# A four-slot PSUM ring, decoding in the units with values, two buffers for R, and the first x in parts: one change to an attention and feed-forward kernel

## The chip, the cores and the metric

The kernel runs on one core of one Trainium2 chip. A core has a matrix engine (TensorE, PE in the profile; PEld is its weight load), VectorE (DVE), ScalarE (ACT), GpSimd (POOL) and SyncE (SP), which here issues DMAs. They run side by side and wait for each other through semaphores. SBUF is the working memory; PSUM takes what PE computes, in 8 banks of 512 float32 a partition, and is read by DVE and ACT.

The metric is the device time of one execution in microseconds. Before the change it is 735.52 us, the median of 3 runs (735.19 to 736.1).

## The reference

Four batches of eight heads of attention, in which a query sees only the keys that fall into the same bucket of a six-bit hash; then a feed-forward block with a convolution along the sequence and a gate:

```python
# q, k, v: (4, 8, 768, 64), proj: (64, 6), w_in: (512, 1024), conv_w: (3, 1024), w_out: (1024, 512)
q_bits = (np.einsum('bhsd,dk->bhsk', q, proj) > 0)      # the same for k; six bits make a bucket
mask = q_bucket[:, :, :, None] == k_bucket[:, :, None, :]
scores = np.where(mask, q @ k.T / 8, -1000000000.0)
attn = np.exp(scores - scores.max(-1))
attn = attn / (attn.sum(-1) + 1e-09)
x = (attn @ v).transpose(0, 2, 1, 3).reshape(B, S, 512)
h = np.maximum(x @ w_in, 0.0)
conv_out = sum(conv_w[k] * hp[:, k:k + S] for k in range(3))   # hp: h with a zero row at each end
return (h * sigmoid(conv_out)) @ w_out
```

[...]

## The kernel before, in words

**Attention.** The 32 heads are taken in 16 pairs (`Pair`). A pair has 12 units (`Unit`): two heads times six tiles of 128 queries. One loop (L460) runs over all 192 units, and four iterations more; with i its index, `pi` is the pair and `k` = 0 to 11 the unit in it. An iteration writes down, in the order in which every engine then executes it:

- PE: the scores s of unit i (`products`, L274; four matmuls, 128 x 768 in two banks), and the transposes t of unit i-4 (`transposes`, L309; six, in two banks).
- DVE: the maximum of unit i (`maximum`, L292), which reads s from PSUM and leaves e in SBUF, and small operations on sums (L303, L296, L306).
- ACT: the copy of t of unit i-4 to SBUF (`to_sbuf`, L319), then the exponential of unit i (L299).
- POOL: the normalisation of unit i-1 (L307). The last matmul of s of unit i waits for the normalisation of unit i-4, so that the transposes behind it find it done.

Every fourth iteration (k = 0, 4, 8) PE also multiplies four units' weights with v (`values`, L322: 24 matmuls into one bank). Its result is copied to SBUF by DVE and stored to a scratch tensor xd in DRAM by the function `out`, which the loop calls in the next iteration, behind that iteration's maximum. This stretch of four units and one v is called a group below.

**The next pair** is prepared in the units k = 1 to 7 of the pair before (`prepare`, L225): POOL splits its R (768 columns of q and k, two heads) into a high and a low part (L198, L203), SP moves the parts to their places, PE computes the hash bits from R (L213, k = 3), DVE and POOL turn them into rows of ones and zeros (L216, L218). R has one buffer: the load of the pair after next, at k = 7, waits until nothing reads the old R.

**PSUM.** s, t and hash take turns in a ring of three slots of two banks (tag S); v, and later h, in a ring of two single banks (tag M). A tile is written only when all that read the slot's previous tile are done.

**Decoding the weights** (`split_weights`, L103) goes on beside attention: 16 blocks of 128 x 512, four DVE steps each (two `upper`, two `lower`), two ACT operations (L86, L132) and three of POOL (L89, L117, L119). From unit 10 on, three of four iterations take one step of it; a block lasts some 11 units. ACT fetches one raw block every six units (L168).

**The feed-forward part** (`feed_forward`, L415) begins in the loop's last iterations. For each of 4 batches, 2 halves of the sequence and 8 chunks f of the inner dimension PE computes h (L350, 12 matmuls), ACT and DVE the Relu, the convolution, the sigmoid and the product (L355 to L363), ACT and POOL split the result in two (L368, L369), and PE, three chunks later, multiplies it with w_out (o, L399, nine matmuls) into three slots of the S ring. Its input x comes back from xd; the four parts of the first batch are loaded at pair 6 and split by POOL (L387, L389) in pairs 9 and 10.

The constants that set this order:

```python
DECODE, RATE = 10, 0.75
FETCH = 6
X0, X0_SPLIT = 6, 9
```

Of the kernel before, what the change touches and what calls it, by code (L numbers as in the profile page):

```python
# [34 lines left out]
PREP_N = 6  # L35
DECODE, RATE = 10, 0.75
FETCH = 6
X0, X0_SPLIT = 6, 9
WC = 512
# [3 lines left out]
def lsh_attention_conv_ffn(ctx, tc, qk, v, hw, w_in, conv_w, w_out, consts, ident_in, out):  # L43
# [5 lines left out]

    turns = {}  # L50

    def ring(pool, bufs, shape, dtype, tag, name):

        k = turns[tag] = (turns.get(tag, -1) + 1) % bufs
        return pool.tile(shape, dtype, tag=f"{tag}{k}", name=name, bufs=1)


# [45 lines left out]
    def split_weights():  # L103

        todo, ends = [], iter(())

        def ahead():  # L110
            if fetched:
                raw, name = fetched.pop(0)
                todo.append(Decode(raw, WC, name))
                todo[-1].size()

        def finish(d, blk):
            nc.gpsimd.tensor_tensor(d.upf, d.upf, blk[:, 0, :].bitcast(F32), ALU.subtract)  # L117
            yield
            nc.gpsimd.tensor_tensor(blk[:, 1, :], d.upf, d.lowf, ALU.add)  # L119

        ahead()
        yield
        todo[-1].clamp()
        yield
        while todo:
            d = todo.pop(0)
            steps = [*d.upper(), *d.lower()]
            for k, step in enumerate(steps):
                step()
                if k == 3:  # L130
                    blk = weights[d.name] = cp.tile([P, 2, WC], F32R, tag=f"w{d.name}", name=f"w{d.name}")
                    nc.scalar.copy(blk[:, 0, :], d.upf)  # L132
                yield
                if k < 2:
                    next(ends, None)
                elif k == 2:
                    ahead()
                elif todo:
                    todo[-1].clamp()
                yield  # L140
            ends = finish(d, blk)

        for _ in ends:
            yield

    def decode_taps(raw):
# [26 lines left out]
    class Pair:  # L173
# [3 lines left out]
        def load(self):  # L177
            nm = self.nm
            self.R = ring(wp, 1, [P, 2, S], F32R, "R", f"R{nm}")
            src = qk[self.b, 2 * self.p:2 * self.p + 2].rearrange("h p s -> p h s")  # L180
            if self.b == self.p == 0:
                for h in range(2):
                    nc.sync.dma_start(self.R[:, h].bitcast(F32), src[:, h])
            else:
                nc.sync.dma_start(self.R.bitcast(F32), src)
            self.Q1 = ring(wp, 2, [P, 2, S], F32R, "Q1", f"Q1{nm}")
            self.K1 = ring(wp, 2, [P, 2, S], F32R, "K1", f"K1{nm}")
            self.Q2, self.K2 = Q2s[self.p % 2], K2s[self.p % 2]
# [18 lines left out]
        def hash(self):  # L207
            hp = ring(ps, 3, [P, 2, 512], F32, "S", f"hash{self.nm}")
            R = self.R.bitcast(F32)
# [23 lines left out]
        def prepare_now(self):  # L233
# [3 lines left out]
            for h in range(2):  # L237
                hps.append(ring(ps, 2, [P, 512], F32, "M", f"hash{nm}_{h}")[:, :HS])
# [29 lines left out]
    class Unit:  # L268
# [5 lines left out]
        def products(self, w):  # L274

            pr, h = self.pair, self.h
            qs = slice(self.t * P, (self.t + 1) * P)
            self.sp = ring(ps, 3, [P, 2, 512], F32, "S", f"s{self.nm}")
            for kk, (A, C) in enumerate(((pr.Q1, pr.K1), (pr.Q2, pr.K2))):
# [29 lines left out]
        def transposes(self):  # L309
            self.tp = ring(ps, 3, [P, 2, 512], F32, "S", f"t{self.nm}")  # L310
            for c in range(NCK):
# [10 lines left out]
    def values(pr, qb, ats):  # L322

        av = ring(ps, 2, [P, 512], F32, "M", f"v{pr.nm}_{qb}")
        for c in range(NCK):
# [11 lines left out]

    g2, prep, acc = [None], [iter(())], []
    xd = [[tc.dram_tile([P, S], F32, name=f"xd{b}_{c}") for c in range(NCC)] for b in range(B)]

    def hidden(b, half, f, xs):
        c0 = 0 if half == 0 else S - HW
        hp = ring(ps, 2, [P, 512], F32, "M", f"h{b}_{half}_{f}")
        n = 0
# [25 lines left out]

    def load_x(b):

        xs = []
        for c in range(NCC):
            if b % 2 == 0:
                x = ring(wp, NCC, [P, 2, S], F32R, "x", f"x{b}_{c}")
            else:
                x = ring(wp, 2, [P, 2, S], F32R, ("Q1", "K1")[c % 2], f"x{b}_{c}")
            nc.sync.dma_start(x[:, 1].bitcast(F32), xd[b][c])
            xs.append(x)  # L380
        return xs

    def split_x(xs):

# [30 lines left out]
    def feed_forward(x0):  # L415

        gs, run, xs, splits = [], [], x0, iter(())
        load_table(AF.Sigmoid)
        todo = [(b, half, f) for b in range(B) for half in range(2) for f in range(NFC)]
        per = 2 * NFC  # L420
        for i in range(len(todo) + FLAG):
            if i % per == 0 and i < len(todo):
                if i:
                    xs = nxt
                if i // per + 1 < B:
                    nxt = load_x(i // per + 1)
                    splits = split_x(nxt)
            if i < len(todo):
                run.append(hidden(*todo[i], xs))
                next(run[i])  # L430
            if 1 <= i <= len(todo):
                next(run[i - 1], None)
            if i == 0:
                acc.extend(ring(ps, 3, [P, 2, 512], F32, "S", f"o{k}") for k in range(3))
            if i >= FLAG:
# [21 lines left out]
    pairs[1].load()  # L457
    n, tail, x0 = len(units), None, None
    outs, av, splits, due = [], None, iter(()), 0
    for i in range(n + LAG + 1):  # L460
# [8 lines left out]
        elif prev:  # L469
            prev.total()  # L470
        for o in outs:
            o()
        outs = []
        if w:
# [11 lines left out]
        if av:  # L486
            outs.append(values(*av))
            av = None
            if i >= n:
                outs.pop()()  # L490
        if burst:
            av = w.pair, w.qb, w.pair.at
        if u and k == PREP + PREP_N and pi + 1 < len(pairs):
            pairs[pi + 1].load_v()
            if pi + 2 < len(pairs):
                pairs[pi + 2].load()
        if i == 3:
            taps.append(decode_taps(cwr))
        for g in taps:
            next(g, None)  # L500
        if i % FETCH == FETCH - 1:
            fetch(1)
        if i >= DECODE:
            due += RATE
            if due >= 1:
                due -= 1
                next(weights_todo, None)
        if pi == X0 and k == 0:
            x0 = load_x(0)
            splits = split_x(x0)  # L510
        if pi >= X0_SPLIT and k % 3 == 2:
            next(splits, None)
        if i == n:
            tail = feed_forward(x0)
        if tail:
            next(tail)
    for o in outs:
        o()
    for _ in tail:
# [44 lines left out]
```

## Time and profile before

| What | Value |
|---|---|
| median of 3 runs | 735.52 us |
| the profiled execution | 732.21 us |
| its span (first to last instruction) | 730.4 us |
| mean granted TensorE clock | 0.993 |
| PE busy | 703.3 us, 96% |
| DVE busy | 497.3 us, 68% |
| ACT busy | 485.6 us, 66% |
| POOL busy | 451.0 us, 62% |
| HBM read and written | 63 GB/s over the span |

The summary of the profile lists the busy time of each engine in 40 equal slices, in tenths:

```profile
PE   5999999999999999999999999999999999999997
DVE  7776767777767777767677764567567666756563
ACT  5778778777778777768777776555455454545553
POOL 4765876876967979996877853365246325622221
```

The first 25 slices are attention, the rest the feed-forward part. All four engines are well loaded in attention.

How to read the rows: a row of a timeline has the start in us from the span's start, the duration in us, the engine, the line, the operation, the tiles (written <- read), their shapes and a count; in square brackets stands how long the engine was idle before and what ended that. A row of a group has the count, the total in us and the mean in ns, then the idle time before such instructions in us. A row of the table of waits has total, times and longest, in us.

### The profile page before, as it was taken

The numbers are of one execution on the slowest core, as the hardware profiler recorded it, in microseconds if no ns is written. First come the engines' busy times: TensorE is split into PE (matmuls) and PEld (weight loads), VectorE is DVE, ScalarE is ACT, GpSimd is POOL, SyncE is SP. The second block draws the span as 40 slices with busy tenths as digits, with TensorE's granted clock in tenths as the row PEclk, the third lists the DMA queues.
The fourth block names the chain that finished last, engine by engine and source line by source line (L and its number), as shares of the span: only waits on it lengthen the run. The fifth ranks groups of instructions, "written<-read, shape, count | busy, mean of one in ns | idle before, by whom it ended". The sixth has DMA issues, their size and how long they took to land.

```text
span 730.4 us, 13371 instructions
## 1 busy us (share of the span) xinstructions
PE 703.3 (96%) x4552; PEld 589.4 (81%) x4552; DVE 497.3 (68%) x1303; ACT 485.6 (66%) x892; POOL 451.0 (62%) x422
## 2 busy tenths in 40 slices
PE   5999999999999999999999999999999999999997
PEld 2877778877877787778777788799989899899896
DVE  7776767777767777767677764567567666756563
ACT  5778778777778777768777776555455454545553
POOL 4765876876967979996877853365246325622221
PEclk7999999999999999999999999999999999999999
DMA  3666676677876555465565512001210120101011
GB/s 115 170 205 184 168 207 190 165 213 215 225 212 190 141 151 159 112 179 159 120 173 158 138 52 99 11 1 44 87 44 15 51 108 1 44 0 44 1 44 43
DMA packets 39572, 84.76 MB, mean 116 GB/s; under 512 B 6960, under 2 KB 14672, under 8 KB 39504
## 3 DMA queue, kind: packets, MB, share of 16 engines
q1 hardware_dynamic: 36912, 75.47, 37.1%
q10 hardware_dynamic: 2592, 8.44, 3.5%
q8 instruction: 36, 0.59, 0.3%
q14 instruction: 32, 0.26, 0.1%
HBM read 33.70 MB, written 12.58 MB: 63 GB/s over the span
## 4 chain that ended last, share of the span: by engine, by line
PE 76%; DVE 10%; DMA 4%; ACT 4%; POOL 3%; issue 2%; SPq 1%; ACTq 0%; POOLq 0%; DVEq 0%
PE o L399 18%; PE h L350 18%; PE v L327 16%; PE s L281 12%; PE t L312 10%; DVE e L292 5%; DMA R<-in_qk 3%; PE hash L213 2%; POOL e L307 2%; ACT at L319 1%; ACT e L299 1%; DMA k<-R 1%; DVE x L332 1%; POOL R L203 1%; DVE ht L359 1%
## 5 line engine op out<-in xcount | busy, mean ns | idle before, releaser
L292 DVE TENSOR_SCALAR_CACHE_REDUCE e<-s 128x768 f32<-128x768 f32 x192 | 182.5, 950 | 84.9 <-PE s L281 84.5
L307 POOL TENSOR_SCALAR e<-e,st 128x768 f32<-128x768 f32 x192 | 186.4, 974 | 86.8 <-DVE st L306 77.5
L319 ACT COPY at<-t 128x768 f32<-128x768 f32 x192 | 152.3, 793 | 87.1 <-PE t L312 87.1
L299 ACT ACTIVATE e<-e,st 128x768 f32<-128x768 f32 x192 | 180.6, 941 | 12.7 <-DVE st L306 7.7
L369 POOL TENSOR_TENSOR g<-ht,g 128x384 fp32r<-128x384 f32 x64 | 69.7, 1089 | 165.8 <-ACT g L368 133.5
L312 PE MATMUL t<-ident,e 128*128 128x128 f32 x1152 | 159.5, 275 | 7.8 <-DVE e L292 4.9
L359 DVE SCALAR_TENSOR_TENSOR ht<-ht,cw 128x384 f32<-128x384 f32 (+1 forms) x128 | 119.3, 932 | 66.9 <-ACT ht L357 64.5
L312 PEld LDWEIGHTS t<-ident,e 128*128 128x128 f32 x1152 | 134.5, 141 | 22.2 <-DVE e L292 15.1
L350 PE MATMUL h<-x,wi 128*128 128x386 f32 x768 | 146.0, 339 | 0.0
L399 PE MATMUL o<-wo,g 128*128 128x512 f32 x576 | 143.6, 394 | 0.0
L350 PEld LDWEIGHTS h<-x,wi 128*128 128x128 f32 x768 | 136.4, 188 | 5.8 <-issue 0.8
L327 PE MATMUL v<-at,v 128*64 128x256 f32 x1152 | 137.0, 383 | 1.6 <-ACT at L319 1.5
L399 PEld LDWEIGHTS o<-wo,g 128*128 128x128 f32 x576 | 107.3, 188 | 20.5
L281 PE MATMUL s<-K,Q 128*128 128x384 f32 x384 | 116.9, 386 | 2.2 <-POOL K L247 1.2
L327 PEld LDWEIGHTS v<-at,v 128*64 128x64 f32 x1152 | 87.4, 137 | 37.7 <-issue 7.9
L281 PE MATMUL s<-k,q 96*128 96x384 f32 x384 | 100.7, 342 | 3.2 <-DVE e L292 2.1
L362 ACT ACTIVATE ht<-ht 128x384 f32<-128x384 f32 x64 | 33.7, 526 | 97.0 <-DVE ht L359 97.0
L281 PEld LDWEIGHTS s<-K,Q 128*128 128x128 f32 x384 | 58.6, 192 | 32.6 <-issue 18.0
L281 PEld LDWEIGHTS s<-k,q 96*128 96x128 f32 x384 | 70.8, 191 | 5.4 <-ACT q L260 3.1
L363 DVE TENSOR_TENSOR ht<-ht 128x384 f32<-128x384 f32 x64 | 47.4, 741 | 33.7 <-ACT ht L362 33.7
L203 POOL TENSOR_TENSOR R<-R,hi 128x768 fp32r<-128x768 f32 x30 | 55.1, 1836 | 0.0
L355 ACT ACTIVATE ht<-h 128x386 f32<-128x386 f32 x64 | 31.6, 495 | 32.6 <-PE h L350 32.6
(65 smaller groups left out, 523.1 us busy)
## 6 DMA issues: line engine op xcount, KB each, us to landing
R<-in_qk SPq DMA_DIRECT2D x15, 768.0 KB
K<-hi SPq DMA_DIRECT2D x60, 192.0 KB
v<-in_v SPq DMA_DIRECT2D x16, 384.0 KB
xd<-x SPq DMA_DIRECT2D x48, 128.0 KB
x<-xd SPq DMA_DIRECT2D x16, 384.0 KB
out<-osb SPq DMA_DIRECT2D x24, 256.0 KB
Q<-hi SPq DMA_DIRECT2D x30, 192.0 KB
q<-hi SPq DMA_DIRECT2D x30, 192.0 KB
```

The source lines that it names most:

```text
L203: nc.gpsimd.tensor_tensor(lo, R, hi.bitcast(F32), ALU.subtract)
L281: mm = nc.tensor.matmul(self.sp[:, half, :HS], A[:, h, qs], C[:, h, half * HS:(half + 1) * HS], start=(kk == 0), stop=(kk == 1))
L292: nc.vector.tensor_scalar(self.e.rearrange("p (a b) -> p a b", a=2), self.sp[:, :, :HS], MASKED, None, ALU.max, ALU.max, accum_out=self.st ...
L299: nc.scalar.activation(self.e, self.e, AF.Exp, bias=self.st[:, 1:2], scale=SCALE, accum_out=self.st[:, 2:3])
L307: self.norm = nc.gpsimd.tensor_scalar(self.e, self.e, self.st[:, 3:4], 0.0, ALU.mult, ALU.add)
L312: nc.tensor.transpose(self.tp[:, c // 3, c % 3 * P:(c % 3 + 1) * P], self.e[:, c * P:(c + 1) * P], ident)
L319: nc.scalar.copy(pr.at[self.h][:, :, :, self.tq * P:(self.tq + 1) * P], self.tp[:, :, :3 * P].rearrange("p j (c q) -> p j c q", c=3))
L327: nc.tensor.matmul(av[h * D:(h + 1) * D, :QB], pr.v[:, c, h, :], ats[h][:, c // 3, c % 3, :], start=(c == 0), stop=(c == NCK - 1), tile_po ...
L350: nc.tensor.matmul(hp[:, :HW], w, x[:, c0:c0 + HW], start=(n == 0), stop=(n == 3 * NCC - 1))
L359: nc.vector.scalar_tensor_tensor(t[:, a:z], ht[:, o + k - 1 + a:o + k - 1 + z], cw[:, f, k:k + 1], t[:, a:z], ALU.mult, ALU.add)
L369: nc.gpsimd.tensor_tensor(g[:, 1, :], t, g[:, 0, :].bitcast(F32), ALU.subtract)
L399: nc.tensor.matmul(op, l, r, start=(f == 0 and i == 0), stop=(f == NFC - 1 and i == 2))
```

## The change

1. The S ring of three and the M ring of two become one ring of four slots of two banks (`slot`). s, t, hash and now v take the slots in turn. The feed-forward part keeps one slot for h (`keep=True`; chunk f uses bank f % 2 of it, so h is one tile from then on), and takes two for o when the first o is due and the third eight chunks later.
2. A block of weights is decoded in 8 units. Both `upper` steps stand in one iteration and both `lower` steps in another four units on, and these are iterations with a v (i a multiple of 4). One raw block is fetched every eight units, three units before it is first used.
3. The copy of v and its store are written down in v's own iteration, behind the decode steps, and not in the next.
4. R has two buffers. The load of the pair after next stands at k = 8, and the load of v at k = 10.
5. The four parts of the first x are loaded one a pair in pairs 10 to 13 (k = 9), and split one a pair in pairs 11 to 14, half at k = 8 and half at k = 10.

The diff, cut to its core:

```diff
-DECODE, RATE = 10, 0.75
-FETCH = 6
-X0, X0_SPLIT = 6, 9
+DECODE = FETCH = 8
+X0 = 10
...
+    slots = list(range(4))
...
+    def slot(name, keep=False):
+
+        k = slots.pop(0)
+        if not keep:
+            slots.append(k)
+        return ps.tile([P, 2, 512], F32, tag=f"S{k}", name=name, bufs=1)
...
         while todo:
             d = todo.pop(0)
-            steps = [*d.upper(), *d.lower()]
-            for k, step in enumerate(steps):
+            for step in d.upper():
                 step()
...
+            ahead()
+            yield
+            if todo:
+                todo[-1].clamp()
+            yield from rest(DECODE // 2 - 1)
+            for step in d.lower():
+                step()
+            blk = weights[d.name] = cp.tile([P, 2, WC], F32R, tag=f"w{d.name}", name=f"w{d.name}")
+            nc.scalar.copy(blk[:, 0, :], d.upf)
+            yield
+            nc.gpsimd.tensor_tensor(d.upf, d.upf, blk[:, 0, :].bitcast(F32), ALU.subtract)
+            yield
+            nc.gpsimd.tensor_tensor(blk[:, 1, :], d.upf, d.lowf, ALU.add)
+            yield from rest(DECODE // 2 - 2)
...
-            self.R = ring(wp, 1, [P, 2, S], F32R, "R", f"R{nm}")
+            self.R = ring(wp, 2, [P, 2, S], F32R, "R", f"R{nm}")
...
-            hp = ring(ps, 3, [P, 2, 512], F32, "S", f"hash{self.nm}")
+            hp = slot(f"hash{self.nm}")
...
-            self.sp = ring(ps, 3, [P, 2, 512], F32, "S", f"s{self.nm}")
+            self.sp = slot(f"s{self.nm}")
...
-            self.tp = ring(ps, 3, [P, 2, 512], F32, "S", f"t{self.nm}")
+            self.tp = slot(f"t{self.nm}")
...
-        av = ring(ps, 2, [P, 512], F32, "M", f"v{pr.nm}_{qb}")
+        av = slot(f"v{pr.nm}_{qb}")[:, 0]
...
-        hp = ring(ps, 2, [P, 512], F32, "M", f"h{b}_{half}_{f}")
+        hp = hps[0][:, f % 2]
...
+        hps.append(slot("h", keep=True))
...
-            if i == 0:
-                acc.extend(ring(ps, 3, [P, 2, 512], F32, "S", f"o{k}") for k in range(3))
+            if i == FLAG:
+                acc.extend(slot(f"o{k}", keep=True) for k in range(2))
+            if i == FLAG + NFC:
+                acc.append(slot("o2", keep=True))
...
-        for o in outs:
-            o()
-        outs = []
...
-        if u and k == PREP + PREP_N and pi + 1 < len(pairs):
+        if u and k == PREP + PREP_N + 1 and pi + 2 < len(pairs):
+            pairs[pi + 2].load()
+        if u and k == PREP + PREP_N + 3 and pi + 1 < len(pairs):
             pairs[pi + 1].load_v()
-            if pi + 2 < len(pairs):
-                pairs[pi + 2].load()
...
-        if i % FETCH == FETCH - 1:
+        if i % FETCH == FETCH - 3:
             fetch(1)
         if i >= DECODE:
-            due += RATE
-            if due >= 1:
-                due -= 1
-                next(weights_todo, None)
-        if pi == X0 and k == 0:
-            x0 = load_x(0)
-            splits = split_x(x0)
-        if pi >= X0_SPLIT and k % 3 == 2:
-            next(splits, None)
+            next(weights_todo, None)
+        if X0 <= pi < X0 + NCC and k == 9:
+            x0.append(load_x(0, pi - X0))
+        if X0 < pi <= X0 + NCC and k in (8, 10):
+            if k == 8:
+                splits = split_x(x0[pi - X0 - 1])
+            next(splits)
+        if out_x:
+            out_x()
+            out_x = None
```

Three places in the built order. The first is DVE around a v of pair 3 of the first batch (iteration i = 40, k = 4), before; e is written by the maximum, wl and wu belong to a decoded block, x is the copy of v:

```order
L292 TENSOR_SCALAR e_3_2_0_1291,st_3_2_0_1290<-s_3_2_0_1285 128x768
L303 TENSOR_SCALAR st_3_1_1_1258<-st_3_1_1_1258 128x1
L296 TENSOR_SCALAR st_3_2_0_1290<-st_3_2_0_1290 128x1
L306 RECIPROCAL st_3_1_1_1258<-st_3_1_1_1258 128x1
L100 TENSOR_SCALAR wli_0_1053<-wui_0_1052 128x512
L292 TENSOR_SCALAR e_3_3_0_1337,st_3_3_0_1336<-s_3_3_0_1331 128x768
L303 TENSOR_SCALAR st_3_2_0_1290<-st_3_2_0_1290 128x1
L296 TENSOR_SCALAR st_3_3_0_1336<-st_3_3_0_1336 128x1
L332 COPY x_2_2_1341<-v_2_2_1317 128x256
L306 RECIPROCAL st_3_2_0_1290<-st_3_2_0_1290 128x1
```

The same place now:

```order
L295 TENSOR_SCALAR e_3_2_0_1299,st_3_2_0_1298<-s_3_2_0_1293 128x768
L306 TENSOR_SCALAR st_3_1_1_1267<-st_3_1_1_1267 128x1
L299 TENSOR_SCALAR st_3_2_0_1298<-st_3_2_0_1298 128x1
L309 RECIPROCAL st_3_1_1_1267<-st_3_1_1_1267 128x1
L101 TENSOR_SCALAR wli_0_1096<-wli_0_1096 128x512
L102 SCALAR_TENSOR_TENSOR wui_0_1095<-rawi_0_1004,wli_0_1096 128x512
L335 COPY x_2_2_1343<-v_2_2_1325 128x256
L295 TENSOR_SCALAR e_3_3_0_1352,st_3_3_0_1351<-s_3_3_0_1346 128x768
```

Two decode steps stand together ahead of the copy of v, and the copy ahead of the next maximum. Before, the next decode step (L101) stood three units on, among the units without a v.

The second place is PE in the third unit after that v, with the semaphores that each row waits for, before:

```order
L281 MATMUL s_3_3_1_1387<-K_3_688,Q_3_687 128x384 [waits Activation_49]
L281 MATMUL s_3_3_1_1387<-K_3_688,Q_3_687 128x384
L281 MATMUL s_3_3_1_1387<-k_1_76,q_1_74 128x384 [waits DMAHW3_49]
L281 MATMUL s_3_3_1_1387<-k_1_76,q_1_74 128x384 [waits Pool_49]
L312 MATMUL t_3_1_1_1397<-ident,e_3_1_1_1259 128x128 [waits DVE_49]
L312 MATMUL t_3_1_1_1397<-ident,e_3_1_1_1259 128x128 x5
L281 MATMUL s_3_4_0_1420<-K_3_688,Q_3_687 128x384 [waits Activation_49]
```

And now:

```order
L284 MATMUL s_3_3_1_1395<-K_3_724,Q_3_723 128x384 [waits DVE_49]
L284 MATMUL s_3_3_1_1395<-K_3_724,Q_3_723 128x384
L284 MATMUL s_3_3_1_1395<-k_1_76,q_1_74 128x384
L284 MATMUL s_3_3_1_1395<-k_1_76,q_1_74 128x384 [waits Pool_49]
L315 MATMUL t_3_1_1_1405<-ident,e_3_1_1_1268 128x128 [waits Activation_49]
L315 MATMUL t_3_1_1_1405<-ident,e_3_1_1_1268 128x128 x5
L284 MATMUL s_3_4_0_1419<-K_3_724,Q_3_723 128x384 [waits DVE_49]
```

Before, s waited for ACT's copy of an earlier t, and t for DVE's maximum of the unit just before. Now s waits for the maximum of the unit two before, and t for ACT's copy of the t two before it.

The third place is SP's queue at the start, before:

```order
L183 DMA R_0_97<-in_qk 128x768 x2
L451 DMA ident<-in_ident 128x128
L192 DMA v_0_103<-in_v 128x768
L454 DMA cwr<-in_conv_w 128x48
L185 DMA R_1_134<-in_qk 128x2x768 [waits DMAHW1_49,DVE_49,DMAHW3_49,PE_49,Activation_49]
```

And now:

```order
L186 DMA R_0_97<-in_qk 128x768 x2
L454 DMA ident<-in_ident 128x128
L195 DMA v_0_103<-in_v 128x768
L457 DMA cwr<-in_conv_w 128x48
L188 DMA R_1_134<-in_qk 128x2x768
```

The load for the second pair waited for three engines and two earlier transfers, and now for nothing.

More of the change, by code (lines that the diff above doesn't have):

```diff
@@ L103, in split_weights @@
     def split_weights():
-        todo, ends = [], iter(())
+        todo = []
         def ahead():
@@ L114, in ahead, with rest @@
                 todo[-1].size()
-        def finish(d, blk):
+        def rest(n):
+            return (None for _ in range(n))
+        ahead()
+        yield
+        todo[-1].clamp()
+        yield from rest(DECODE - 1)
+        while todo:
+            d = todo.pop(0)
+            for step in d.upper():
+                step()
+            ahead()
+            yield
+            if todo:
+                todo[-1].clamp()
+            yield from rest(DECODE // 2 - 1)
+            for step in d.lower():
+                step()
+            blk = weights[d.name] = cp.tile([P, 2, WC], F32R, tag=f"w{d.name}", name=f"w{d.name}")
+            nc.scalar.copy(blk[:, 0, :], d.upf)
+            yield
             nc.gpsimd.tensor_tensor(d.upf, d.upf, blk[:, 0, :].bitcast(F32), ALU.subtract)
@@ L119, in finish @@
             nc.gpsimd.tensor_tensor(blk[:, 1, :], d.upf, d.lowf, ALU.add)
[L121 to L126, printed above, removed]
-            steps = [*d.upper(), *d.lower()]
-            for k, step in enumerate(steps):
[L129 to L144, printed above, removed]
+            yield from rest(DECODE // 2 - 2)
     def decode_taps(raw):
@@ L237, in prepare_now @@
             for h in range(2):
-                hps.append(ring(ps, 2, [P, 512], F32, "M", f"hash{nm}_{h}")[:, :HS])
+                hps.append(slot(f"hash{nm}_{h}")[:, 0, :HS])
                 for g in range(4):
@@ L335, in values @@
         return out
-    g2, prep, acc = [None], [iter(())], []
+    g2, prep, acc, hps = [None], [iter(())], [], []
     xd = [[tc.dram_tile([P, S], F32, name=f"xd{b}_{c}") for c in range(NCC)] for b in range(B)]
@@ L369, in hidden, with load_x, split_x @@
         nc.gpsimd.tensor_tensor(g[:, 1, :], t, g[:, 0, :].bitcast(F32), ALU.subtract)
[L371 to L383, printed above, removed]
+    def load_x(b, c):
+        if b % 2 == 0:
+            x = ring(wp, NCC, [P, 2, S], F32R, "x", f"x{b}_{c}")
+        else:
+            x = ring(wp, 2, [P, 2, S], F32R, ("Q1", "K1")[c % 2], f"x{b}_{c}")
+        nc.sync.dma_start(x[:, 1].bitcast(F32), xd[b][c])
+        return x
+    def split_x(*xs):
         for x in xs:
@@ L425, in feed_forward @@
                 if i // per + 1 < B:
-                    nxt = load_x(i // per + 1)
-                    splits = split_x(nxt)
+                    nxt = [load_x(i // per + 1, c) for c in range(NCC)]
+                    splits = split_x(*nxt)
             if i < len(todo):
@@ L457, in lsh_attention_conv_ffn @@
     pairs[1].load()
-    n, tail, x0 = len(units), None, None
-    outs, av, splits, due = [], None, iter(()), 0
+    n, tail, x0 = len(units), None, []
+    out_x, av, splits = None, None, iter(())
     for i in range(n + LAG + 1):
@@ L486, in lsh_attention_conv_ffn @@
         if av:
-            outs.append(values(*av))
+            out_x = values(*av)
             av = None
-            if i >= n:
-                outs.pop()()
         if burst:
             av = w.pair, w.qb, w.pair.at
-        if u and k == PREP + PREP_N and pi + 1 < len(pairs):
+        if u and k == PREP + PREP_N + 1 and pi + 2 < len(pairs):
+            pairs[pi + 2].load()
+        if u and k == PREP + PREP_N + 3 and pi + 1 < len(pairs):
             pairs[pi + 1].load_v()
-            if pi + 2 < len(pairs):
-                pairs[pi + 2].load()
         if i == 3:
@@ L516, in lsh_attention_conv_ffn @@
             next(tail)
-    for o in outs:
-        o()
     for _ in tail:
```

## The prediction

> **What bounds the kernel now.** I read the summary first (the table above), then the timeline of single engines in the attention stage, then the chain of waits, then the table of waits. PE looks full in the summary, but the ends of its rows are modelled, so its share hides gaps. The question is how far its pace lies from the densest pace that it shows. One group of four units (scores s and transposes t each, then one product with the values, v) runs like this where nothing holds it up, PE alone:
>
> ```profile
> 192.91 2.81 PE L327 MATMUL v<-at,v 128*64 128x256 f32 x24
> 195.65 0.61 PE L281 MATMUL s<-K,Q 128*128 128x384 f32 x2
> 196.10 0.51 PE L281 MATMUL s<-k,q 96*128 96x384 f32 x2
> 196.45 0.82 PE L312 MATMUL t<-ident,e 128*128 128x128 f32 x6
> 197.03 0.60 PE L281 MATMUL s<-K,Q 128*128 128x384 f32 x2
> ...
> 201.34 2.00 PE L327 MATMUL v<-at,v 128*64 128x256 f32 x16
> ```
>
> Start to start, v takes 2.74 us, s 0.80, t 0.58, and v returns after 201.34 - 192.91 = **8.43 us**. The v rows of the chain of waits give the real pace:
>
> ```profile
> 27.30 2.74 PE v L327 x24
> ...
> 119.54 2.74 PE v L327 x24
> 128.91 2.74 PE v L327 x24
> ...
> 438.63 2.80 PE v L327 x24
> ```
>
> There are 48 v (16 pairs, three each). From the first to the 46th are 45 intervals in 411.33 us, 9.14 each. Fourteen of them hold the hash of the next pair; one of those, among the shortest, is 128.91 - 119.54 = 9.37. At the dense pace the 45 would take 31 x 8.43 + 14 x 9.37 = 392.5. So **18.8 us** is all that better overlap can win here. Who holds PE up:
>
> ```profile
> PEld t L312 <- DVE e L292: 15.1, 24, 1.6
> ...
> PE hash L213 <- DMA R<-in_qk: 2.4, 3, 1.3
> ```
>
> The columns are total, times and longest, in us; PEld is the weight load, which meets a stall first. Transposes that wait for the maximum of the unit before are by far the greatest of these waits. One such place, all engines:
>
> ```profile
> 78.19 0.41 DVE L332 COPY x<-v 128x256 f32<-128x256 f32 x1
> ...
> 78.56 1.28 POOL L119 TENSOR_TENSOR wi<-wui,wli 128x512 fp32r<-128x512 f32 x1
> 78.59 1.54 DVE L100 TENSOR_SCALAR wli<-wui 128x512 int32<-128x512 int32 x1
> ...
> 81.06 0.33 PE L312 MATMUL t<-ident,e 128*128 128x128 f32 x1 [1.26 <-DVE e L292]
> ```
>
> A decode step, itself held beside a POOL operation that began just before it, sits on DVE ahead of a maximum. The maximum is late, and the transposes that take over its slot in the ring of three stand for 1.26 us.
>
> The feed-forward stage, from some 465 us, is another matter:
>
> ```profile
> 469.86 2.10 PE o L399 x9
> 471.96 2.12 PE h L350 x12
> ```
>
> ```profile
> ACT ht L355 <- PE h L350: 32.6, 61, 2.1
> ```
>
> PE alternates h and o without a gap, and ACT waits for PE 61 times. Nothing can be won there.
>
> **The change part by part.** No instruction goes or comes: each engine has as many rows in the order as before. Only places and waits differ.
>
> *Ring of four.* Before, transposes waited for the maximum one unit back: 0.58 + 0.80 = 1.38 us of PE work lie between, and DVE needs 0.94 plus what is queued ahead of it. Now scores wait for the maximum two units back, with 0.58 + 0.80 + 0.58 = 1.96 between, and every second pair of transposes for a copy of ACT, with 2.18 between. The v shares the ring, and waits for DVE or ACT work at least as old.
>
> *Decoding beside v.* DVE's free time around a v, where no decode lies:
>
> ```profile
> 439.72 0.17 DVE L306 RECIPROCAL st<-st 128x1 f32<-128x1 f32 x1
> 442.38 0.96 DVE L292 TENSOR_SCALAR_CACHE_REDUCE e<-s 128x768 f32<-128x768 f32 x1 [2.50 <-PE s L281]
> ```
>
> It is free for 2.49 us. The copy of v (0.41 at 78.19) now stands ahead of the next maximum and can begin when v is done; so two decode steps have 2.49 - 0.41, about 2.1 us. Their price, by the dearer group of each line of a block's first half:
>
> ```profile
> L95 DVE SCALAR_TENSOR_TENSOR wui<-rawi,wli 128x512 int32<-128x512 int32 x8 | 10.2, 1279 | 0.0
> ...
> L94 DVE TENSOR_SCALAR wlo<-wlo 128x512 int32<-128x512 int32 x8 | 5.8, 721 | 3.4 <-POOL wlo L89 3.4
> ```
>
> That half costs 1.28 + 0.72 = 2.00; the other half, two operations of the same kinds and shape, I take at the same. It fits, barely, and these means hide a spread:
>
> ```profile
> 193.90 2.18 DVE L95 SCALAR_TENSOR_TENSOR wui<-rawi,wli 128x512 int32<-128x512 int32 x1
> ```
>
> This one took 0.9 more than its line's mean. Such a step late in v's shadow delays the next maximum, exponential and copy, and v itself. The Trainium skill, "SBUF — State Buffer", section "Who interferes with whom", has a rule for it: DVE and GpSimd share one pair of ports, and whichever starts second is blocked until the other's instruction ends. The rows at 78.56 and 78.59 agree with it. By that rule both steps of a unit could be held in turn; if that happened in every unit as at 78.59, the sum below would be +12 instead of -16.5, which is the slower rival.
>
> I take 0.1 us lost in each of the 32 units with decoding (16 blocks, two halves): **3.2 us** given back. The low bound is nothing, since the means fit; the high one is the slower rival's 32.
>
> ACT's part of decoding (one operation of a block's two in such a unit) falls into ACT's idle time at v:
>
> ```profile
> 197.31 0.80 ACT L319 COPY at<-t 128x768 f32<-128x768 f32 x1 [2.09 <-PE t L312]
> ...
> 200.55 0.79 ACT L319 COPY at<-t 128x768 f32<-128x768 f32 x1
> ```
>
> 2.09 us hide an operation on 512 columns, where the copy of 768 takes 0.80: nothing. The raw block is now fetched three units ahead of its first use, some 5 us at the 3.24 us that ACT takes from its copy at 197.31 to the second next at 200.55. If it came later, the remaining 1.3 us of idle time would still cover it; beyond that each us costs 16, once a block.
>
> *Two buffers for R.* The load for pair 1 no longer waits for the first pair's reads:
>
> ```profile
> 12.69 0.39 SPq L185 DMA_DIRECT2D R<-in_qk  x1
> ...
> 16.97 1.51 PE L213 MATMUL hash<-R,hw_sb 128*32 128x384 f32 x8 [1.27 <-DMA R<-in_qk]
> ```
>
> It is now free to be issued right behind the first loads, some 9 us earlier, and lands, by the same 4.28 us, long before the hash: **-1.3 us**, between 0 (another wait behind it) and 2. Later loads lose the wait for their predecessor's DMAs; what that wins (the 2.4 us of the DMA row above) lies within the 18.8.
>
> *x a part a pair.* Splits move from pairs 9 and 10, where they met decoding, to pairs 11 to 14, two POOL operations a pair. What this wins is in the 18.8 too. What hides the splits is the distance of four units between a unit's scores and its transposes; where POOL ran so late that this was used up, the split of a part would cost some 2 us by the POOL operation on two inputs of the same size (1.28 for 512 columns, so 1.9 for 768), 8 for the four.
>
> *One tile for both halves of h.* In the built order h now waits for the Relu of the chunk just before, not of the one before that. The transition, where no o stands between them yet:
>
> ```profile
> 460.31 0.49 ACT L355 ACTIVATE ht<-h 128x386 f32<-128x386 f32 x1
> ...
> 464.74 2.81 PE L327 MATMUL v<-at,v 128*64 128x256 f32 x22 [1.54 <-ACT at L319]
> ```
>
> In the steady stage the o between two h (2.10) covers a Relu of 0.49, which starts as h ends: nothing. Here the fourth h would start after 460.31 + 0.49 = 460.8 instead of earlier; with h 2.12 and o 2.10 behind it the last v starts near 465.1 instead of 464.74: **+0.4 us**, because v waited there anyway.
>
> Sum: -18.8 + 3.2 - 1.3 + 0.4 = **-16.5 us**. The profiled execution took 732.21 us, of which the span is 730.4; it would become 715.7. The median of the timed runs, 735.52, lies 3.3 above it, so the forecast in their terms is 735.52 - 16.5 = **719.0 us**.
>
> **The rivals.** *ACT takes DVE's place.* In the dense group above, the third copy ends at 200.55 + 0.79 = 201.34, just as v starts, and v needs it. PE cannot outrun ACT there, and whatever delays the first exponential of a group delays v as much. For it: no slack at all. Against it: 8.43 was reached while decoding was in progress. At 0.25 us a group it takes back 45 x 0.25 = 11.3: 730.3 us.
>
> *The decoding jams v.* Both steps of every unit with decoding start just behind a POOL operation and take 1.54 us, as at 78.59. Together 3.1 us, they overrun the 2.1 by 1.0, 32 times: 32 us against a gain of 19.7 without the 3.2, so 735.5 + 12.3 = 748 us. The kernel gets slower from a mean of 2.1 + 19.7 / 32 = 2.7 us a unit. For it: in the built order POOL has its split of R, its longest operation in a pair, in the unit ahead of two of a pair's three v. Against it: the same steps beside the same POOL work average 2.0 now. The rule of "SBUF — State Buffer" in the Trainium skill that is weighed above speaks for this rival; the row at 78.59 bears it out for a single step only.
>
> *The stalls only move.* If PE waits for POOL's normalisation or for SP's transfers instead, the time stays at 735.5. Against it: the table of waits names few of either.
>
> **How the numbers follow.** Forecast, 712 to 724: 0.64. ACT takes over, 724 to 734: 0.20. Stalls move, within 734 to 737: 0.06. Jam, over 737: 0.10. The low end of the range is the full 18.8 + 1.3 and 2 us more from shorter hash intervals, 713; the high end takes in the rival of ACT with 2 us to spare, 732. Outside are the jam, the unmoved time and thin edges, 0.2 in all. A measurement of this kernel can tell about 0.2%, 1.5 us, from no change; by that, faster 0.84, same 0.06, slower 0.10.
>
> **What would show it.** Right: the waits of t for DVE e fall from 15.1 us to under 4; v returns every 8.4 to 8.6 us, and 9.4 with a hash; the two decode steps stand between the reciprocal and the copy of v and together take about 2 us; the second load of R is issued near 3 us and no hash waits for it; h and o keep 2.12 and 2.10. Wrong: waits of v for ACT's copy in tenths of a us per group (first rival); decode rows near 2 us each with v late behind them (jam); waits of s for POOL e grow (third). If the feed-forward stage stretched, the reading of the shared h tile would be wrong.

## The result, and the profile after

| | before | after |
|---|---|---|
| median | 735.81 us (735.19 to 736.13, 4 runs) | 723.37 us (722.6 to 724.71, 4 runs) |
| ratio, 95% interval | | 0.9843 (0.9821 to 0.9866) |
| the profiled execution | 732.21 us | 723.74 us |
| its span | 730.4 us | 722.0 us |
| first v starts | 27.23 us | 26.36 us |
| 31 intervals from v to v without a hash | 273.6 us, 8.83 each | 262.8 us, 8.48 each |
| 14 intervals with a hash | 137.7 us, 9.84 each | 140.6 us, 10.04 each |
| from the 47th v to the end of the span | 284.0 us | 284.4 us |

The last four rows are taken from the starts of v on PE's timeline and make up the span, but for the one interval from the 46th v to the 47th, 7.8 us in both. They are used for every kernel below: *dense* are the intervals without a hash, *hash groups* those with one.

Now line 284 is the scores, 295 the maximum, 315 the transposes, 322 ACT's copy of them, 330 v, 335 the copy of v, and 101 to 108 are the decode steps on DVE, which turn the two 32-bit words of each float64 weight into float32 parts. The timeline of PE after the change, v alone:

```profile
26.36 3.15 PE L330 MATMUL v<-at,v 128*64 128x256 f32 x24
...
44.55 2.81 PE L330 MATMUL v<-at,v 128*64 128x256 f32 x24
52.90 2.37 PE L330 MATMUL v<-at,v 128*64 128x256 f32 x19
...
114.72 3.29 PE L330 MATMUL v<-at,v 128*64 128x256 f32 x24
124.99 2.81 PE L330 MATMUL v<-at,v 128*64 128x256 f32 x24
...
429.79 2.94 PE L330 MATMUL v<-at,v 128*64 128x256 f32 x24
```

A dense group is now as short as 52.90 - 44.55 = 8.35. But a hash group stands at 124.99 - 114.72 = 10.27, where the shortest of its kind take 9.35. The 45 intervals sum to 403.4 us, against 411.3. The table of waits, weight loads and matmuls:

```profile
PEld v L330 <- ACT at L322: 2.9, 8, 0.6
...
PEld t L315 <- DVE bits L219: 0.2, 1, 0.2
```

```profile
PE s L284 <- DMA Q<-R: 1.9, 2, 1.6
...
PE s L284 <- DMA k<-R: 1.0, 2, 0.6
```

The 15.1 us of transposes that waited for a maximum are gone; the only wait of t for DVE left is 0.2 us. Grown are the waits of v for ACT's copy: from their start to the next scores the first 46 v take 132.3 us, and before the change 126.9. Where nothing holds a v it takes 2.74. New are waits of scores for the low parts of R. The second kind, PE and then SP's queue in one place:

```profile
172.45 0.82 PE L315 MATMUL t<-ident,e 128*128 128x128 f32 x6
174.88 0.59 PE L284 MATMUL s<-K,Q 128*128 128x384 f32 x2 [1.61 <-DMA Q<-R]
176.10 0.62 PE L284 MATMUL s<-k,q 96*128 96x384 f32 x2 [0.63 <-DMA k<-R]
```

```profile
163.77 0.71 SPq L225 DMA_DIRECT2D q<-bits  x1
164.59 0.45 SPq L336 DMA_DIRECT2D xd<-x  x1
165.49 0.53 SPq L204 DMA_DIRECT2D Q<-hi  x1
166.07 0.58 SPq L204 DMA_DIRECT2D q<-hi  x1
166.70 1.52 SPq L204 DMA_DIRECT2D K<-hi  x2
168.33 0.88 SPq L208 DMA_DIRECT2D Q<-R  x1
169.25 0.86 SPq L208 DMA_DIRECT2D k<-R  x1
170.16 0.59 SPq L188 DMA_DIRECT2D R<-in_qk  x1
```

POOL has had this low part since 163.48 (the row of L206 further down). SP issues it only at 168.33, behind eight DMAs of bits (the last is shown), a store and four DMAs of the high part; the scores wait for it until 174.88. Low parts that SP issues 2.2 to 5.8 us after POOL had them lie behind every second pair (the odd ones, from pair 1 to pair 11). Against 9.35, these six hash groups are 9.3 us too long in sum. Of that, 3.2 us are v's wait for ACT's copy, 0.4 to 0.7 in each. Behind pairs 1 and 11 it is nearly all of the excess, and no score waits for a low part there; the other 6.1 us lie behind pairs 3, 5, 7 and 9.

### The profile page after: what moved, and what is told of

Its sections match the earlier page's. It is cut to its first block, busy times and chain, and to the rows that moved or that the text cites. A ratio compares the mean times of both kernels' runs of the same rounds, so it can differ in the third digit from the quotient of the medians.

```text
span 722.0 us, 13429 instructions
## 1 busy us (share of the span) xinstructions
PE 702.4 (97%) x4552; PEld 598.8 (83%) x4552; DVE 523.1 (72%) x1303; ACT 485.5 (67%) x892; POOL 449.6 (62%) x422
## 4 chain that ended last, share of the span: by engine, by line
PE 86%; DVE 3%; DMA 3%; ACT 3%; POOL 2%; issue 2%; SPq 0%; POOLq 0%; ACTq 0%; DVEq 0%
PE h L353 19%; PE o L399 19%; PE s L284 17%; PE v L330 16%; PE t L315 14%; DMA k<-R 3%; PE hash L216 2%; ACT e L302 1%; POOL e L310 1%; DVE e L295 1%; ACT at L322 1%; POOL R L206 1%; DMA R<-in_qk 0%; DVE Q L254 0%; DVE k L259 0%
## 5 line engine op out<-in xcount | busy, mean ns | idle before, releaser
L310 POOL TENSOR_SCALAR e<-e,st 128x768 f32<-128x768 f32 x192 | 181.5, 949 | 82.8 <-PE s L284 31.9
L372 POOL TENSOR_TENSOR g<-ht,g 128x384 fp32r<-128x384 f32 x64 | 69.4, 1084 | 166.4 <-ACT g L371 134.0
L315 PE MATMUL t<-ident,e 128*128 128x128 f32 x1152 | 157.2, 272 | 0.0
L353 PE MATMUL h<-x,wi 128*128 128x386 f32 x768 | 146.0, 339 | 1.9 <-ACT ht L358 1.9
L315 PEld LDWEIGHTS t<-ident,e 128*128 128x128 f32 x1152 | 137.5, 140 | 6.7 <-DVE bits L219 0.2
L330 PE MATMUL v<-at,v 128*64 128x256 f32 x1152 | 141.8, 384 | 0.2 <-ACT at L322 0.2
L330 PEld LDWEIGHTS v<-at,v 128*64 128x64 f32 x1152 | 96.3, 137 | 32.1 <-ACT at L322 2.9
L206 POOL TENSOR_TENSOR R<-R,hi 128x768 fp32r<-128x768 f32 x30 | 59.8, 1992 | 0.0
L306 DVE TENSOR_SCALAR st<-st 128x1 f32<-128x1 f32 x192 | 29.1, 152 | 33.4 <-ACT e L302 29.2
```

Of the source, the lines that this page charges most:

```text
L206: nc.gpsimd.tensor_tensor(lo, R, hi.bitcast(F32), ALU.subtract)
L310: self.norm = nc.gpsimd.tensor_scalar(self.e, self.e, self.st[:, 3:4], 0.0, ALU.mult, ALU.add)
L315: nc.tensor.transpose(self.tp[:, c // 3, c % 3 * P:(c % 3 + 1) * P], self.e[:, c * P:(c + 1) * P], ident)
L330: nc.tensor.matmul(av[h * D:(h + 1) * D, :QB], pr.v[:, c, h, :], ats[h][:, c // 3, c % 3, :], start=(c == 0), stop=(c == NCK - 1), tile_po ...
L353: nc.tensor.matmul(hp[:, :HW], w, x[:, c0:c0 + HW], start=(n == 0), stop=(n == 3 * NCC - 1))
L372: nc.gpsimd.tensor_tensor(g[:, 1, :], t, g[:, 0, :].bitcast(F32), ALU.subtract)
```

## The experiments

Each kernel was run beside the kernel before; ratios are to those runs. The last two columns are sums of the profiled execution, in us.

| kernel | median, us | ratio (95% interval) | dense | hash |
|---|---|---|---|---|
| before, profiled again | 734.25 (1 run) | | 274.0 | 139.3 |
| before + ring | 739.30 | 1.0078 (1.0062 to 1.0095) | 277.6 | 140.1 |
| before + ring + early copy of v | 732.61 | 0.9965 (0.9943 to 0.9987) | 267.2 | 141.8 |
| before + R twice | 729.87 | 0.9939 (0.9919 to 0.9960) | 273.6 | 137.5 |
| before + ring + early copy + R twice | 723.46 | 0.9857 (0.9816 to 0.9897) | 266.6 | 137.1 |
| **changed kernel** | 723.37 | 0.9843 (0.9821 to 0.9866) | 262.8 | 140.6 |
| changed, R once | 740.50 | 1.0081 (1.0067 to 1.0095) | 265.0 | 155.5 |
| changed, decoding as before | 721.09 | 0.9806 (0.9773 to 0.9840) | 265.1 | 135.2 |
| changed, R loaded earlier | 725.77 | 0.9881 (0.9859 to 0.9903) | 262.5 | 146.0 |
| changed, POOL's decode steps later | 726.64 | 0.9875 (0.9844 to 0.9906) | 264.9 | 142.3 |
| changed, fetches as before | 723.98 | 0.9856 (0.9817 to 0.9895) | 262.8 | 141.5 |
| changed, v a unit later | **714.90** | 0.9721 (0.9688 to 0.9754) | 261.4 | 133.4 |
| the same, fetches as before | 716.65 | 0.9760 (0.9724 to 0.9796) | 262.7 | 132.9 |

**The kernel before, profiled again.** No edit.

> The kernel before, once more, for its profile. Its first profiled execution took 732.21 us, 3.3 below the median of its timed runs, while that of the changed kernel (723.74) stands at its median. If the first profile was of an unusually short execution, this one takes 734.5 to 736 and its 45 intervals between v and v sum to 413 or more (first profile: 411.3); if profiled executions of this kernel are always shorter than timed ones, it takes 732 to 733 again.

734.25 us, just under the first range, with 413.3 us in the 45 intervals. So the first profile was of a short execution, 2.0 us of it in these intervals. Differences of single profiles below some 2 us are not read.

**The ring alone.** The kernel before, with `slot` for s, t, hash, v, h and o as in point 1 of the change, and nothing else.

> The kernel before with the four-slot PSUM ring alone (and the one tile for both halves of h and the later accumulators that come with it); decoding, R, fetches and x as before. If the waits of t for DVE were the ring's, as the prediction has it, nearly all of the gain is here or shared with decoding: 722 to 729, with the waits of t for e under 5 us. If decoding beside v is what removed them, the ring alone gives less than 3 us: 732 to 736.

It is slower than before, which neither side expected. All waits of t for a late maximum are gone, yet every dense group takes 8.86 or more. One of them, DVE and PE (in this kernel line 341 is the copy of v, 321 the transposes):

```profile
208.38 0.41 DVE L341 COPY x<-v 128x256 f32<-128x256 f32 x1
```

```profile
207.68 0.59 PE L290 MATMUL s<-K,Q 128*128 128x384 f32 x2
208.11 0.51 PE L290 MATMUL s<-k,q 96*128 96x384 f32 x2
208.94 0.85 PE L321 MATMUL t<-ident,e 128*128 128x128 f32 x6 [0.32 <-DVE st L315]
```

In a ring of four, the fourth tile behind v takes v's slot, and that is this t. In the old order the copy of v stands behind the next maximum and ends at 208.79; t starts at 208.94. The table of waits has 45 such waits, under the name of a reciprocal that stands nearby:

```profile
PE t L321 <- DVE st L315: 14.2, 45, 0.3
```

A releaser is inferred; the slot tells which it is, and the next run tests it.

**Ring and early copy.** The same, and in the loop:

```diff
-        for o in outs:
-            o()
-        outs = []
         if w:
             w.transposes()
...
+        for o in outs:
+            o()
+        outs = []
         if i == n:
```

> The kernel before with the four-slot ring and with v's result copied right behind v, not in the unit behind it; decoding, R, fetches and first x as before. With the ring alone every dense group took 8.86 to 8.88 us, and in it the t that takes v's slot waited for that copy (the copy ended 208.79, t began 208.94). If this wait is what the ring costs, the dense groups return to 8.35 to 8.6 and the kernel takes 720 to 729. If the ring is slow for another reason, or DVE's decoding holds t anyway, it stays at 735 to 740.

Dense groups fall by 10.4 us, to 8.62 each, just above the 8.6 expected; the total, 732.61, lies between the two expected ranges. Below the ring lies another limit. The group of the hash's matmuls in this kernel (x120 | busy, mean | idle before and what ended it):

```profile
L222 PE MATMUL hash<-R,hw_sb 128*32 128x384 f32 x120 | 13.4, 519 | 8.8 <-DMA R<-in_qk 5.6 <-DVE st L315 2.2 <-DVE st L305 0.9
```

and one place of it, PE and SP:

```profile
206.59 0.82 PE L321 MATMUL t<-ident,e 128*128 128x128 f32 x6
209.45 0.85 PE L222 MATMUL hash<-R,hw_sb 128*32 128x384 f32 x8 [2.04 <-DMA R<-in_qk]
```

```profile
202.90 0.39 SPq L194 DMA_DIRECT2D R<-in_qk  x1
```

R's load waited on SP for its only buffer until 202.90, so the hash waits for it. Before the change 2.4 us of waits for R had shown in all.

**R twice, with and without the ring.** One edit, to the kernel before and to the last one:

```diff
-            self.R = ring(wp, 1, [P, 2, S], F32R, "R", f"R{nm}")
+            self.R = ring(wp, 2, [P, 2, S], F32R, "R", f"R{nm}")
```

> The kernel before with two buffers for R alone. If the late R and the waits of t for DVE lie one behind the other, each hiding the other's gain, R alone gives little beyond the start's 1 us: 730 to 734, the waits of t for DVE staying near 15 us. If R is the gain by itself, and adds to the ring's, it takes 721 to 726.

> The kernel before with the four-slot ring, v's result copied right behind v, and two buffers for R (its load still in the seventh unit of a pair, before the low parts of the second head); decoding, fetches and first x as before. Ring and copy alone gave a ratio of 0.9965, and their hash groups waited 5.6 us for R by the table of waits and 10 to 11.6 us stood where 9.4 is dense. If R's wait for its buffer is the limit that the ring lays bare, this takes 719 to 724, as the changed kernel with the old decoding did (721.09). If the later loads of R and v or x a part a pair made that difference, it stays at 729 to 733.

Alone it gives 4.6 us (734.45 to 729.87, just under the first expected range), and the waits of t for a maximum stay. Where the 4.6 us lie cannot be seen: its profile is of its slowest execution, 732.15, with 411.1 us in the 45 intervals, as in the first profile of before, and the first v at 27.42.

```profile
PEld t L312 <- DVE e L292: 17.2, 26, 1.7
```

On top of ring and copy it gives 732.61 - 723.46 = 9.1 us. The ring and the copy are worth 2.1 us alone (734.71 to 732.61) and 6.4 on top of R (729.87 - 723.46). So each limit seems to hide a part of what the other's removal is worth. How much is uncertain: the kernel with ring and copy ran on another chip than the two with R twice, and by the ratios, each to the kernel before on its own chip, R gives some 4.5 us alone and 7.9 on top, a difference no larger than the intervals leave open. The hash groups of the profiles point the same way: 137.7 and 139.3 before against 137.5 with R alone, but 141.8 against 137.1 on top of ring and copy. With these three edits the kernel is as fast as the changed one: the new decoding, the later loads and x in parts give nothing together that can be measured.

**The changed kernel with R once.** The same line, the other way round.

> The changed kernel with R in one buffer again, its load still at the eighth unit of a pair. Theory: in the changed kernel the early load of R (768 KB) runs beside the transfers of the low parts that the next pair's second head waits for, and this makes the hash groups of every second pair 0.7 to 3.1 us too long, 9.3 us in all. Then with the load held until those transfers have landed, the hash groups' excess falls from 9.3 to below 4 us, the start gives back 0.9 to 1.3, and the kernel takes 717 to 721. Rival: the low parts come late because GpSimd and SP's queue are late with them; then the excess stays near 9 and with the start given back the time is 724 to 726.

740.5, far from both. The collision of which the text speaks was not the point. With one buffer the load, which the change puts behind the low parts (k = 8), leaves at 180.88 in the place of the 170.16 above, and the hash waits for it:

```profile
PE hash L216 <- DMA R<-in_qk: 14.5, 8, 3.2
```

With the load at this place 17 us hang on the second buffer, more than the whole gain of the change. The start gave nothing back: the first v starts at 26.29, and with two buffers at 26.36.

**Decoding as before, in the changed kernel.** `split_weights`, RATE, DECODE and FETCH from the kernel before.

> The changed kernel with decoding as before (one DVE step at a time, in three of four units, from the eleventh unit on, a fetch every six units); ring, R and x as changed. If decoding beside v is a part of its own, a step of 0.7 to 1.3 us now stands between a maximum and the next again, the waits of t or s for DVE come back in part, and the kernel takes 727 to 733. If the ring and the early copy of v's result do all of it, it takes 721 to 725.

721.09: the second case, and if anything faster than with the new decoding. No wait of t for DVE comes back in its table of waits, so the ring removed them, not the place of decoding. Decoding beside v makes dense groups 2.3 us shorter and hash groups 5.4 longer. The later loads and x in parts were run only together, never each by itself.

**What lengthens every second pair's hash group.** Three single edits to the changed kernel: R's load at k = 3; POOL's two steps of a block two units later; a fetch every six units.

```diff
-        if u and k == PREP + PREP_N + 1 and pi + 2 < len(pairs):
+        if u and k == 3 and pi + 2 < len(pairs):
             pairs[pi + 2].load()
```

> The changed kernel with the load of R moved five units ahead, to the fourth unit of a pair, which the second buffer allows; the issue then stands on SP's queue away from the low parts. Theory of the collision: the excess of the hash groups falls from 9.3 to below 3 us and the kernel takes 715 to 718. Rival (GpSimd and SP's queue are late, or the fetch of raw weights and the load of v collide instead): 722 to 724.

```diff
-            yield
+            yield from rest(DECODE // 2 - 1)
             nc.gpsimd.tensor_tensor(d.upf, d.upf, blk[:, 0, :].bitcast(F32), ALU.subtract)
             yield
             nc.gpsimd.tensor_tensor(blk[:, 1, :], d.upf, d.lowf, ALU.add)
-            yield from rest(DECODE // 2 - 2)
```

> The changed kernel with GpSimd's two steps of a decoded block (difference and sum, 1.3 us each) two units later. Moving R's load did not shorten the hash groups of every second pair; in these the two steps stand between R's high part and its low part of the first head, push that low part back by 2 us, with it the hash bits, whose eight DMA issues of 0.7 to 0.8 us then hold the second head's parts in SP's queue until 3 to 5 us after GpSimd has them ready. Two units later the steps stand behind the low part in every pair. If that is the cause, the hash groups' excess over 9.35 falls from 9.3 to under 3 us and the time to 715 to 718. Rival (the fetch of raw weights, which in these pairs falls beside the low parts, delays the transfers): 722 to 724.

```diff
-        if i % FETCH == FETCH - 3:
+        if i % 6 == 5:
```

> The changed kernel with the raw weights fetched every six units, as before, which puts no fetch (512 KB) beside the low parts of a pair's second head; decoding, ring, R and x as changed. The low parts land 4.2 to 5.1 us after their issue in the pairs with such a fetch, and 2.6 to 3.0 in all others, by the records of the transfers; the pair behind the last fetch is the one exception of its kind (2.64). If the fetch is the cause, the low parts land in 3 us throughout, the hash groups' excess over 9.35 falls from 9.3 to 2 to 4 us and the time to 716 to 719. If lateness of GpSimd and SP's queue is the larger part, it stays at 721 to 724.

None of them removes it, and none makes the kernel faster; two are slower than either expectation. The excess of the six hash groups over 9.35 was 9.3 us; it is 13.4 with R early (7.4 of it in one interval), 7.5 with POOL's steps later (and then five of the other hash groups grow by 0.7 each) and 9.8 with the old fetches. But where the fetches have ended the excess is small: 0.66 behind pair 11 of the changed kernel, 0.45 and 0.65 behind pairs 9 and 11 with the old fetches, which end earlier. So a late low part and a fetch seem to be needed together. Behind pair 1 of the changed kernel a fetch ran beside the low part too, and no score waited; there the low part left SP 2.2 us after POOL had it, behind the other odd pairs 3.4 us or more. The old rhythm of fetches did not avoid the meeting either: with it a low part was issued at 169.56, packets of a fetch began at 171.5, and the scores waited until 176.34. That is read from the traces; no run isolates it.

**v a unit later.** In the changed kernel, and then with a fetch every six units as well (`hold` is False at first):

```diff
-        if av:
+        if av and (hold or i >= n):
             out_x = values(*av)
             av = None
+        hold = bool(av)
```

> The changed kernel with the matmuls of v one unit later, behind the t of the next unit. Theory (the prediction's first rival in small): v's second matmul waits for ACT's copy of the last transposes, 0.1 to 0.6 us in 46 groups, 6.3 us in all; with a unit between the copy and v this wait goes, the dense groups stay at 8.35 and the kernel takes 716 to 719. Rival: ACT and DVE behind v are as late as before, and the wait turns up at the next s or t: 722 to 725.

> The changed kernel with v one unit later and the raw weights fetched every six units. The first alone took 714.9; in it the groups lost 2.4 us behind every second pair and some 2 elsewhere to the fetch. If both gains add, 711 to 714; if what v gained was the same wait, 714 to 716.

714.90 us, the fastest of all and below the expected range. PE, one hash group:

```profile
194.32 2.81 PE L330 MATMUL v<-at,v 128*64 128x256 f32 x24
197.06 0.61 PE L284 MATMUL s<-K,Q 128*128 128x384 f32 x2
197.51 0.52 PE L284 MATMUL s<-k,q 96*128 96x384 f32 x2
```

From v to the next scores it is 2.74 us, the bare length of v; over all 46 places the sum falls from 132.3 us to 126.4. The excess behind odd pairs, of which v's wait is a part, falls from 9.3 to 2.4. The 45 intervals take 394.8 us, 8.6 less, which is the gain. Of it 7.2 lie in the hash groups. In the dense ones 2.7 us of v's wait go and only 1.4 are won; the rest turns up elsewhere. The fetches of the second run add nothing: 716.65 is above both of its ranges.

Where v had waited for ACT, the chain begins at decoding. DVE and POOL of the changed kernel in the group ahead of the place shown first (v ran from 159.93 for 3.01 us):

```profile
161.31 0.50 DVE L107 TENSOR_SCALAR wli<-wui 128x512 int32<-128x512 int32 x1
161.84 2.19 DVE L108 SCALAR_TENSOR_TENSOR wli<-rawi,wli 128x512 f32<-128x512 uint32 x1
163.96 0.41 DVE L335 COPY x<-v 128x256 f32<-128x256 f32 x1
164.29 0.94 DVE L295 TENSOR_SCALAR_CACHE_REDUCE e<-s 128x768 f32<-128x768 f32 x1
```

```profile
161.49 1.99 POOL L206 TENSOR_TENSOR R<-R,hi 128x768 fp32r<-128x768 f32 x1
```

The second step takes 2.19 us beside a POOL operation that began just before it, and ends 0.55 after that one. So the copy of v starts 1.0 us after v's end; the maximum, the exponential and ACT's copies follow late, and the next v meets the last copy. A unit between copy and v takes that up. This is one place, and decoding is not the only reason: with decoding as before, the same 46 places sum to 135.6 us, more than the 132.3 here.

## Why the prediction came near, point by point

- **The total.** 719.0 was forecast, 723.37 came; the range held it. The time was 4.4 us above the forecast. Of the 16.5 us forecast, 12.4 came by the medians; by the spans of the profiles it is 8.4, or 10.5 against the second profile of before. That the total came so near owes something to the wide range, 713 to 732, and to luck in the terms below.
- **The 18.8 us of late maxima: mis-sized, and it was two things.** The prediction set all 45 intervals to the dense pace. The 31 dense ones did reach it: 261.3 forecast (31 x 8.43), 262.8 measured. The 14 hash groups did not: 131.2 forecast (14 x 9.37), 140.6 measured, more than before. This is the step that failed. Of these 9.4 us, 5.4 go when decoding is as before (135.2). Hash groups depend on R, on POOL and on SP's queue, not on the ring, which alone left them at 140.1; the rows of late maxima said nothing of them.
- **The ring as the cause of the gain.** It does remove the waits of t, as predicted. But what waits for v's slot was left out; the sentence that v "waits for DVE or ACT work at least as old" looks at v's own wait only. Alone the ring costs some 5 us. It pays only with point 3 of the change, which the prediction used for DVE's time and nothing else.
- **Two buffers for R.** Priced at 1.3 us at the start, the later loads as part of the 18.8 by the 2.4 us of the DMA row. Measured: 4.6 us alone, 9.1 on top of ring and copy, both by medians. The wait in the profile of before was small, it seems, because the late maxima kept PE behind R: with ring and copy the same wait was 5.6 us.
- **The start.** Forecast -1.3, measured 27.23 to 26.36, -0.9, but not for the reason given. The load leaves early, as said, and no hash waits for it:

```profile
3.06 0.43 SPq L188 DMA_DIRECT2D R<-in_qk  x1
```

Yet with R once the changed kernel starts its first v at 26.29, though its load leaves at 12.63 and the hash waits 1.49 us; and with R twice alone the first v starts at 27.42, since a transpose ahead of it waits 1.38 us for DVE instead. So in these profiles the second buffer moved the hash and not the first v, and that the number fits is luck.

- **Decoding, 3.2 us given back.** With decoding as before the changed kernel is 2.3 us faster by the medians, 3.1 in the intervals (5.4 in the hash groups, less 2.3 in the dense ones); the size fits, though the intervals of the two ratios overlap. The working did not: the lower half was taken at the upper half's 2.00 us.

```profile
L108 DVE SCALAR_TENSOR_TENSOR wli<-rawi,wli 128x512 f32<-128x512 uint32 x8 | 12.0, 1504 | 0.3
...
L107 DVE TENSOR_SCALAR wli<-wui 128x512 int32<-128x512 int32 x8 | 8.7, 1084 | 0.0
```

By these two rows it takes 1504 + 1084 ns, or 2.59 us, of a window of 2.1. The rule of the Trainium skill that was weighed ("SBUF — State Buffer", "Who interferes with whom") fits the pair of rows at 161.49 and 161.84; the rival built on it, over 737 us, did not come: single units took from 1.72 us to 3.18, where it had 3.1 in every one.
- **ACT takes DVE's place.** Given 0.20 and 11.3 us. v did come to wait for ACT's copy: beyond the bare 2.74 the first 46 v take 6.3 us, before 0.8. Moving v away from it won 8.5 us, not all of which was this wait. It lay beside the forecast, not in its place.
- **The stalls only move.** As a whole wrong, for the hash groups right: their waits went from R and late maxima to the low parts and to ACT's copy.
- **The h tile, x in parts, the last stage.** From the 47th v to the end 284.0 became 284.4, the +0.4 forecast. The h at the transition does wait for its Relu, 0.66 and 1.26 us; but kernels with the same h tile take 284.1 (ring alone) to 284.7, so the size itself is within their scatter. The rest of the feed-forward stage has the same pace. No run isolates x in parts.
- **The step from the profile to the runs.** Adding 3.3 us was right for the kernel before; the second profile at 734.25 shows that its first was short. It also means that the 18.8 was counted from a short execution.

Open is which share of the odd pairs' excess is POOL's, SP's and the fetch's: three edits that took one away each left it, two that changed the rhythm as a whole (decoding spread, v later) removed most of it.

## What to carry to other kernels

When tiles are put into a common ring, list for every tile who takes its slot next and what must be read before that; the reader's place in the order is part of the edit. When a table of waits names one big releaser, give a second limit its own sum, worked out at the faster pace: here the wait for R grew once PE was no longer behind it, and by the medians each of the two edits alone was worth less than it was with the other. A consumer placed right behind its producer's last copy takes every jitter of that producer; here one unit of distance won two thirds as much as the whole change.

## What the runs showed of the hardware

A wait of PE costs more than its length once it is long. The kernel with the fetches as before waits 2.48 us for a low part, until 176.34. By windows of 2 us (the busy time of PE, PEld, DVE, ACT and POOL, each with its count, then the granted clock, the third number from the end):

```profile
174.00:176.00 2.00, 0.00 (x0) 0.00 (x0) 0.47 (x5) 1.62 (x3) 0.91 (x1) 1.00 1.04 228
176.00:178.00 2.00, 1.32 (x6) 0.99 (x7) 0.08 (x1) 0.00 (x0) 0.00 (x0) 0.95 0.99 330
178.00:180.00 2.00, 2.00 (x10) 2.00 (x9) 1.15 (x5) 0.78 (x2) 0.83 (x1) 0.50 0.75 284
180.00:182.00 2.00, 2.00 (x16) 1.33 (x14) 1.23 (x5) 1.39 (x4) 1.63 (x3) 0.70 0.47 105
```

Read from these windows, the clock falls to half some 1.5 us after the wait and stays there for about 3.4 us: 2 x (0.05 + 0.50 + 0.30) = 1.7 us of work at full clock are lost on top of the wait. With R loaded early a wait of 3.89 us cost more: windows of 0.57, 0.50, 0.50 and 0.72 from 178 on, 3.4 us lost, and that one interval took 16.76 us. After waits of 1.61 us (changed kernel) and 2.04 us (ring and early copy) the clock stayed at 1.00. In the changed kernel with R once it stayed so after 2.16 us, and fell to 0.50 after 2.45 and 3.23 us, and after one wait of 2.24 us that had a wait of 1.08 some 5 us ahead of it. The Trainium skill, "TensorE: Matmul & The Clock Gate", section "HAM oscillation — how this bites in real kernels", warns of idle gaps of more than about 3.4 us; here 2.48 us were enough.
